# A window-attention kernel: new lead-in, an instruction order that counts tiling changes, deadlines for the small jobs, and the final add on GpSimd

## The chip, the core and the metric

The kernel runs on one core of one Trainium2 chip. The metric is the device time of one execution in microseconds; before the change it was 1138.44 us (median of three runs, 1138.19 to 1139.52). The profiles are single executions; their span (first to last instruction) is about two microseconds shorter than the time of the same execution.

## The reference

The image has 224 x 224 tokens of 96 channels. Half of the channels attend in horizontal stripes of 8 rows, the other half in vertical stripes of 8 columns: 28 + 28 windows of 1792 tokens, 48 channels each.

```python
qkv = jnp.einsum('bhwc,cd->bhwd', x, wqkv)
q, k, v = (qkv[..., :C].copy(), qkv[..., C:2 * C].copy(), qkv[..., 2 * C:].copy())
...
ah = _softmax(jnp.einsum('bqc,bkc->bqk', qh, kh) * scale, axis=-1)   # 28 horizontal windows
oh = jnp.einsum('bqk,bkc->bqc', ah, vh).reshape(B, H, W, C2)
...
av = _softmax(jnp.einsum('bqc,bkc->bqk', qv, kv) * scale, axis=-1)   # 28 vertical windows
...
return jnp.einsum('bhwc,cd->bhwd', o, wo)      # o: oh in the first 48 channels, ov in the others
```

## The kernel before

Two windows are computed side by side (a pair): 14 horizontal pairs, then 14 vertical ones. Every pair has 49 score tiles of 128 x 1024, so there are 1372. Each is made by PE (QK, in 64-row tiling, two windows x two column halves), turned into weights by either ACT (one exponential) or DVE (five instructions that build the bits of a bfloat16 exponential), and used by PE (PV, in 128-row tiling). PE also does the "fills": projections to K, Q and V, and the output projection. DVE copies their results out of PSUM ("evacuates" them), where the kernel has one tensor, `ps`, that PE writes and that is used in eight parts of 512 columns, the banks; only the first pair's Q goes through ACT.

The kernel has no dynamic scheduling. While it is built, a small model of the engines (`add` with an occupancy for each instruction) plays the program through and decides the order on each engine, including which tile goes to DVE. The order is then frozen; on the chip every engine works through its own list, waiting where a semaphore tells it to.

```python
        def add(eng, waits, fn, occ=100.0, done=None):
            ...
            start = max([now[0], tfree[eng]] + [vis(w) for w in waits])
            tfree[eng] = start + occ
            ...
        # ACT: one tile
            e = add("act", [ev, bufA_ev[sl]], lambda e, base=base, sl=sl: e.activation(
                PTA[sl][:], ps[:, base * 512:(base + 2) * 512], ACTF.Exp, scale=LN2 / 128.0), 912.0, 1200.0)
        # DVE: one tile, five steps; steps 1 and 3 are fp16 multiplies of two SBUF tiles
            if k == 0:
                return lambda e: e.tensor_scalar(tt_sb[:], dps.bitcast(U16)[:, 0:2048:2], CS / 65536.0, CS * CA3, ALU.mult, ALU.add)
            if k == 1:
                return lambda e: e.tensor_tensor(sq_sb[:], tt_sb[:], tt_sb[:], ALU.mult)
            if k == 2:
                return lambda e: e.tensor_scalar(sq_sb[:], sq_sb[:], CB, None, ALU.add)
            if k == 3:
                return lambda e: e.tensor_tensor(tt_sb[:], sq_sb[:], tt_sb[:], ALU.mult)
            return lambda e: e.scalar_tensor_tensor(PTD[sl][:].bitcast(U16), dps, CC, tt_sb[:], ALU.add, ALU.add)
        # PE takes another job only if it is over before the next QK for ACT can start
            def fits(occ):
                return nextfree is None or t + occ <= nextfree + SLACK or nextfree - t > 1500.0
        # last step of a vertical window, for each of up to five 128-token pieces s, on DVE
                            return e.scalar_tensor_tensor(out_sb[b][:, wdw, k0 + s, :], bk3[:, s, 0:C], rci[:, s:s + 1],
                                                          Ph_sb[:, k0 + s, j, :], ALU.mult, ALU.add)
```

The softmax here doesn't subtract the row's maximum and nothing guards it: scores larger than these inputs give would overflow.

## Time and profile before

Lines of the page of the kernel before. A group's line gives: source line, engine, operation, tiles, shape, count, then busy time and the mean length of one instruction in ns, then the engine's idle time just before them and what ended it. PEclk is the granted PE clock in tenths of full speed, in 40 slices of the span.

```profile
span 1137.3 us, 27720 instructions
...
PE 1023.0 (90%) x11824; PEld 372.9 (33%) x11824; DVE 1088.1 (96%) x2024; ACT 1110.5 (98%) x1206; POOL 1.6 (0%) x9
...
PEclk9999999999999999999999999999999999999999
...
ACT 68%; DVE 20%; PE 9%; SPq 2%; issue 1%; DMA 0%; DVEq 0%
...
L731 ACT ACTIVATE PTA<-ps 128x1024 bf16<-128x1024 f32 x1200 | 1106.6, 1087 | 7.9 <-PE ps L587 6.0
...
L742 DVE TENSOR_SCALAR tt_sb<-ps 128x1024 f16<-128x1024 uint16 x172 | 209.6, 1219 | 12.5 <-PE ps L587 10.8
L749 DVE SCALAR_TENSOR_TENSOR PTD<-ps,tt_sb 128x1024 uint16<-128x1024 f32 x172 | 209.7, 1219 | 1.9
...
L748 DVE TENSOR_TENSOR tt_sb<-sq_sb,tt_sb 128x1024 f16<-128x1024 f16 x172 | 118.5, 689 | 3.6
L744 DVE TENSOR_TENSOR sq_sb<-tt_sb 128x1024 f16<-128x1024 f16 x172 | 117.6, 684 | 0.8
...
L521 DVE SCALAR_TENSOR_TENSOR out_sb<-ps,rc,Ph_sb 128x96 bf16<-128x96 f32 x392 | 96.8, 308 | 1.0
L746 DVE TENSOR_SCALAR sq_sb<-sq_sb 128x1024 f16<-128x1024 f16 x172 | 72.2, 420 | 1.6
```

The five groups with count 172 are the five steps of the DVE tiles; L521 is the final step, five instructions in a row for a group of pieces. ACT is busy for 98% of the span and DVE for 96%. Lengths overlap in the pipeline: an exponential is listed with 1087 ns, but in the trace the most frequent distance from the start of one to the start of the next is 904 ns, which is ACT's real pace here.

The first exponentials, from the timeline of ACT (start, length of the merged stretch, how many):

```profile
14.75 0.64 ACT L392 ACTIVATE QT_sb<-ps,biasq 128x448 bf16<-128x448 f32 x1 [12.51 <-PE ps L369]
15.79 1.82 ACT L392 ACTIVATE QT_sb<-ps,biasq 128x448 bf16<-128x448 f32 x3 [0.40 <-PE ps L369]
17.55 1.94 ACT L731 ACTIVATE PTA<-ps 128x1024 bf16<-128x1024 f32 x2
19.78 1.94 ACT L731 ACTIVATE PTA<-ps 128x1024 bf16<-128x1024 f32 x2 [0.29 <-PE ps L587]
24.61 1.02 ACT L731 ACTIVATE PTA<-ps 128x1024 bf16<-128x1024 f32 x1 [2.89 <-PE ps L587]
26.18 12.08 ACT L731 ACTIVATE PTA<-ps 128x1024 bf16<-128x1024 f32 x13 [0.54 <-PE ps L587]
```

Nothing is exponentiated before 17.55 us, since all K and Q of the first pair are made first, and four microseconds later ACT runs dry again.

A split: the span is (number of exponentials) x 0.904 us plus the time ACT lost. The loss of one interval is the distance between two starts less 0.904 us, summed over the single instructions of the trace. For before: 1200 x 0.904 = 1084.8; until the first exponential 17.6; gaps up to 60 us 7.1; later intervals over 0.935 us lose 18.9, shorter ones 3.4; after the last 5.4. Sum 1137.2.

### The profile page before, as it was taken

The numbers are of one execution on the slowest core, as the hardware profiler recorded it, in microseconds if no ns is written. First come the engines' busy times: TensorE is split into PE (matmuls) and PEld (weight loads), VectorE is DVE, ScalarE is ACT, GpSimd is POOL, SyncE is SP. The second block draws the span as 40 slices with busy tenths as digits, with TensorE's granted clock in tenths as the row PEclk, the third lists the DMA queues.
The fourth block names the chain that finished last, engine by engine and source line by source line (L and its number), as shares of the span: only waits on it lengthen the run. The fifth ranks groups of instructions, "written<-read, shape, count | busy, mean of one in ns | idle before, by whom it ended". The sixth has DMA issues, their size and how long they took to land.

```text
span 1137.3 us, 27720 instructions
## 1 busy us (share of the span) xinstructions
PE 1023.0 (90%) x11824; PEld 372.9 (33%) x11824; DVE 1088.1 (96%) x2024; ACT 1110.5 (98%) x1206; POOL 1.6 (0%) x9
## 2 busy tenths in 40 slices
PE   5898899999999999999998898999899989999987
PEld 1333333333333333333333333333333333333332
DVE  3899999999999999999999999999999999999997
ACT  3999999999999999999999999999999999999998
POOL 0000000000000000000000000000000000000000
PEclk9999999999999999999999999999999999999999
DMA  4311011101100110110111222222122222221111
GB/s 83 54 34 34 10 26 34 34 1 33 35 19 16 33 34 5 30 31 16 21 34 33 40 42 40 38 41 41 38 40 42 40 40 43 40 39 26 19 27 25
DMA packets 169124, 37.31 MB, mean 33 GB/s; under 512 B 169000, under 2 KB 169000, under 8 KB 169000
## 3 DMA queue, kind: packets, MB, share of 16 engines
q1 hardware_dynamic: 167384, 35.36, 16.2%
q8 instruction: 92, 1.51, 0.6%
q10 hardware_dynamic: 1616, 0.18, 0.1%
q14 instruction: 32, 0.26, 0.1%
HBM read 0.15 MB, written 9.63 MB: 9 GB/s over the span
## 4 chain that ended last, share of the span: by engine, by line
ACT 68%; DVE 20%; PE 9%; SPq 2%; issue 1%; DMA 0%; DVEq 0%
ACT PTA L731 68%; PE ps L587 4%; DVE tt_sb L742 4%; PE ps L691 3%; DVE out_sb L521 3%; DVE PTD L749 3%; DVE sq_sb L744 2%; DVE tt_sb L748 2%; SPq L143 2%; DVE QT_sb L396 1%; DVE sq_sb L746 1%; DVE OT_sb L759 1%; DVE KT_sb L420 1%; DVE Ph_sb L482 1%; PE ps L369 1%
## 5 line engine op out<-in xcount | busy, mean ns | idle before, releaser
L731 ACT ACTIVATE PTA<-ps 128x1024 bf16<-128x1024 f32 x1200 | 1106.6, 1087 | 7.9 <-PE ps L587 6.0
L587 PE MATMUL ps<-QT_sb,KT_sb 49*64 49x512 bf16 (+3 forms) x6272 | 540.6, 370 | 81.3 <-ACT PTA L731 71.6
L691 PE MATMUL ps<-PTA,V_sb 128*64 128x512 bf16 (+1 forms) x2734 | 405.4, 365 | 1.4 <-DVE V_sb L337 0.4
L587 PEld LDWEIGHTS ps<-QT_sb,KT_sb 49*64 49x64 bf16 (+1 forms) x6272 | 157.1, 104 | 453.2 <-ACT PTA L731 382.8
L742 DVE TENSOR_SCALAR tt_sb<-ps 128x1024 f16<-128x1024 uint16 x172 | 209.6, 1219 | 12.5 <-PE ps L587 10.8
L749 DVE SCALAR_TENSOR_TENSOR PTD<-ps,tt_sb 128x1024 uint16<-128x1024 f32 x172 | 209.7, 1219 | 1.9
L691 PEld LDWEIGHTS ps<-PTA,V_sb 128*64 128x64 bf16 x2734 | 119.0, 108 | 150.0 <-issue 129.5
L748 DVE TENSOR_TENSOR tt_sb<-sq_sb,tt_sb 128x1024 f16<-128x1024 f16 x172 | 118.5, 689 | 3.6
L744 DVE TENSOR_TENSOR sq_sb<-tt_sb 128x1024 f16<-128x1024 f16 x172 | 117.6, 684 | 0.8
L369 PE MATMUL ps<-xT_sb,w_sb 128*64 128x448 bf16 (+1 forms) x448 | 85.5, 381 | 18.6 <-DMA xT_sb<-in_x_dram 9.9
L521 DVE SCALAR_TENSOR_TENSOR out_sb<-ps,rc,Ph_sb 128x96 bf16<-128x96 f32 x392 | 96.8, 308 | 1.0
L746 DVE TENSOR_SCALAR sq_sb<-sq_sb 128x1024 f16<-128x1024 f16 x172 | 72.2, 420 | 1.6
L396 DVE TENSOR_SCALAR QT_sb<-ps,biasq 128x448 bf16<-128x448 f32 x108 | 73.0, 676 | 0.4
L759 DVE CAST OT_sb<-ps 128x512 bf16<-128x512 f32 x112 | 68.9, 616 | 3.5 <-PE ps L691 3.5
L691 PE MATMUL ps<-PTD,V_sb 128*64 128x512 bf16 (+1 forms) x402 | 66.8, 353 | 2.7 <-DVE QT_sb L396 2.3
L420 DVE TENSOR_SCALAR KT_sb<-ps,shift 128x448 bf16<-128x448 f32 x84 | 56.6, 676 | 1.8 <-PE ps L369 1.6
L337 DVE CAST V_sb<-ps 128x480 bf16<-128x480 f32 (+1 forms) x84 | 51.5, 615 | 2.2 <-PE ps L330 2.2
L482 DVE TENSOR_TENSOR Ph_sb<-ps,rc 128x480 bf16<-128x480 f32 x84 | 52.0, 619 | 1.1
L369 PEld LDWEIGHTS ps<-xT_sb,w_sb 128*64 128x64 bf16 (+1 forms) x448 | 25.3, 108 | 72.5 <-issue 25.6
L471 PE MATMUL ps<-wo_sb,OT_sb 128*64 128x97 bf16 x784 | 33.0, 212 | 2.5 <-DMA wo_sb<-one_sb 1.6
L510 PE MATMUL ps<-wo_sb,OT_sb 128*128 128x97 bf16 x392 | 32.9, 210 | 2.2 <-DVE OT_sb L759 1.2
L330 PE MATMUL ps<-w_sb,xT_sb 128*128 128x48 bf16 (+1 forms) x784 | 34.1, 185 | 0.7 <-DVE V_sb L337 0.4
(33 smaller groups left out, 168.1 us busy)
## 6 DMA issues: line engine op xcount, KB each, us to landing
out_dram<-out_sb SPq DMA_DIRECT2D x389, 24.0 KB, 1.9
xT_sb<-in_x_dram SPq DMA_TRANSPOSE x336, 2.5
w_sb<-in_wqkv_dram ACTq DMA_DIRECT2D x2, 54.0 KB, 2.9
out_dram<-out_sb ACTq DMA_DIRECT2D x3, 24.0 KB, 1.9
wo_sb<-in_wo_dram SPq DMA_DIRECT2D x4, 9.0 KB
wo_sb<-one_sb SPq DMA_DIRECT2D x4, 0.0 KB
```

The lines of the kernel that those rows point to most:

```text
L369: ins = e.matmul(o, lhsT=wS[0:kr, wblk(P, kind), :], rhs=x_cols(wdw), start=True, stop=True)
L396: return e.tensor_scalar(q_dst, q_src(bk), QS, biasq[:, 0:1], ALU.mult, ALU.add)
L521: return e.scalar_tensor_tensor(out_sb[b][:, wdw, k0 + s, :], bk3[:, s, 0:C], rci[:, s:s + 1], Ph_sb[:, k0 + s, j, :], ALU.mult, ALU.add)
L587: ins = e.matmul(bank(base + wdw)[64 * kh:64 * kh + 64, i * qs:(i + 1) * qs], lhsT=KT_sb[b][r0:r0 + kk, kt * 128 + 64 * kh:kt * 128 + 64 * ...
L691: ins = e.matmul(bk[64 * wdw:64 * wdw + 64, 0:qs], lhsT=V_sb[b][:, wdw, kt, :], rhs=pt[:, wdw * 512 + i * qs:wdw * 512 + (i + 1) * qs], st ...
L731: e = add("act", [ev, bufA_ev[sl]], lambda e, base=base, sl=sl: e.activation(PTA[sl][:], ps[:, base * 512:(base + 2) * 512], ACTF.Exp, sca ...
L742: return lambda e: e.tensor_scalar(tt_sb[:], dps.bitcast(U16)[:, 0:2048:2], CS / 65536.0, CS * CA3, ALU.mult, ALU.add)
L744: return lambda e: e.tensor_tensor(sq_sb[:], tt_sb[:], tt_sb[:], ALU.mult)
L746: return lambda e: e.tensor_scalar(sq_sb[:], sq_sb[:], CB, None, ALU.add)
L748: return lambda e: e.tensor_tensor(tt_sb[:], sq_sb[:], tt_sb[:], ALU.mult)
L749: return lambda e: e.scalar_tensor_tensor(PTD[sl][:].bitcast(U16), dps, CC, tt_sb[:], ALU.add, ALU.add)
L759: ev = add("dve", [e_pv], lambda e: e.tensor_copy(OT_sb[b][:, q0:q0 + qs], bank(bi)[:, 0:qs]), t_ps(qs), t_ps(qs) + 150.0)
```

## The change

The intent: start the exponentials sooner; take the final add from DVE, which is as full as ACT, so that it can take more tiles; make the order model truer, so that gaps of ACT close. The core of the diff (cut):

```diff
+    SWITCH = 100.0
+    SLACK = 120
+    PACE = 1
+    FDUE = 25.0
+    DSLACK = 300.0
...
+            if mode is not None:
+                if mode != pe_mode[0]:
+                    start += SWITCH
+                pe_mode[0] = mode
+            if eng == "act" and start > tfree[eng]:
+                start += 17.0
...
-        for i in range(8):
+        for i in range(12):          # warm-up matmuls
...
+                    cuts = [0, 512, NTOK] if P == 0 else [k * 448 for k in range(5)]
...
-                q0, qs = c * PCH, PCH
+                q0, qs = (CH_Q0[c], CH_SIZES[c]) if P == 0 else (c * PCH, PCH)
...
-                return Fill(waits, pe_fn, 50.0 * n + 40.0, [dict(fn=ev_fn, occ=t_ps(n * C2))], post,
+                return Fill(waits, pe_fn, 25.0 * n, [dict(fn=ev_fn, occ=t_ps(n * C2))], post,
...
+                    def d2(e, bk):
+                        return e.tensor_tensor(tmpi[:, 0:n, :], bk3[:, 0:n, 0:C],
+                                               rci[:, 0:n].unsqueeze(2).to_broadcast([128, n, C]), ALU.mult)
...
+                        def d3(e):
+                            return e.tensor_tensor(out_sb[b][:, wdw, k0:k0 + n, :], tmpi[:, 0:n, :],
+                                                   Ph_sb[:, k0:k0 + n, j, :], ALU.add)
+                        if tail[0]:
+                            ev = add("dve", ow, d3, t_ps(n * C), t_ps(n * C) + 90.0)
+                        else:
+                            ev = add("pool", ow, d3, 2.3 * n * C + 150.0)
...
-            def fits(occ):
-                return nextfree is None or t + occ <= nextfree + SLACK or nextfree - t > 1500.0
-
-            if D["cur"] is None and fits(245.0):
+            def fits(occ, mode="r128", slack=SLACK):
+                if mode != pe_mode[0]:
+                    occ += SWITCH
+                if mode != "r64":
+                    occ += SWITCH
+                return nextfree is None or t + occ <= nextfree + slack or nextfree - t > 1500.0
+
+            if D["cur"] is None and fits(240.0, "r64", DSLACK):
...
-            late = want_fill and progress() > f.target + 2 and used < NBA - 1
+            late = want_fill and progress() > f.due - 10 and used < NBA - 1
...
-                PTA[sl][:], ps[:, base * 512:(base + 2) * 512], ACTF.Exp, scale=LN2 / 128.0), 912.0, 1200.0)
+                PTA[sl][:], ps[:, base * 512:(base + 2) * 512], ACTF.Exp, scale=LN2 / 128.0), 904.0, 1195.0)
...
-                    for i, f in enumerate(seq):
-                        f.target = P * NG + 1 + i * (NG - 14.0) / len(seq)
+                    for i, f in enumerate(order):
+                        f.target = P * NG + PACE * i
+                        f.due = P * NG + NG - LOOK - 18 + 2 * i
```

## The prediction

> **What bounds it now.** The page: ACT 1110.5 us busy (98% of 1137.3) and DVE 1088.1 (96%); PE is at 90%. The chain of waits is 68% the exponential on ACT. There are 1372 score tiles: 1200 go to ACT, 172 to DVE. Start to start in the trace, an exponential takes 904 ns at best; a DVE tile takes about 3.98 us over its five instructions. The span splits into 1200 x 0.904 = 1084.8 us, plus 52.5 us in which ACT lacks work:
> - lead-in: first exponential at 17.55 us, and about 7 us of gaps before 60 us (PE stood on the second pair's x);
> - steady part: about 22 us of small gaps (some 130 intervals over 0.95 us);
> - tail: 5.2 us after the last exponential.
>
> **Costs of the change.**
> 1. Lead-in. K and Q of the first pair wait for two transposes, not all. A transpose takes the queue 1.3 us at 448 tokens and 1.4 at 224, so nearly a fixed cost (estimate): the first pieces are issued by 3.3 us and land near 5.5 (eight landed at 12.6). Twelve warm-up matmuls at 0.43 us hold PE to about 6.6 us and become the limit. From the first K matmul to the first exponential the dependent work is about 2.6 us (4.9 now, as all K and Q came first): first exponential near 9.2 us. Lead-in loss falls from about 24.5 to 12.5 us.
> 2. Final add. On DVE 392 instructions (96.8 us; 1.21 a group of five) become 92 multiplies, 480 wide as a rule; the same shape takes 0.57 us in the first phase. DVE saves about 44 us and loses some 3 to the first pair (Q there, OT in pieces). GpSimd gets some 85 adds[...].
> 3. Order model with tiling changes, deadlines, earlier QK for DVE: ACT gaps in the steady part fall from 22 to about 15 us, DVE idles about 5 us less.
>
> **Sum.** ACT and DVE share the tiles, so DVE time is worth only 0.904/(3.98+0.904) = 0.185 us a us; an ACT gap 0.815. With non-tile DVE time (work and idle) going from 452 to about 410 us, and ACT loss from 52.5 to about 33: 1.227 T = 1240.3 + 33 + 0.227 x 410, T = 1113.5 us of span, about 176 DVE tiles; the time is 1 us more.
>
> **Prediction:** 1114 us, 1103 to 1124; faster by over 2%: 0.55, within 2%: 0.44, slower: 0.01.
>
> **What would show it.** First exponential at 8-10.5 us; 174 to 182 DVE tiles; multiply near 0.6 us; [...]intervals of the exponential over 950 ns clearly fewer; the fp16 instructions longer in the second half only where GpSimd overlaps.
>
> **What would make it wrong.** GpSimd locking DVE out (few more tiles, fp16 steps over 1 us); a 1280-token transpose whose cost grows with size (K of the rest after 11 us); the new order filling more gaps than I think (1105).

Parts of step 2 and one sign are cut: how long one of GpSimd's adds takes, and with it how long GpSimd would be busy; which DVE steps its reads would hold up; and a booking for that, 12 us of DVE loss, possibly 0 to 40. None of them was worked out from a trace or a run; the 12 us was a guess, and it was noted then that no run had shown the loss. The sum came to a span of T = 1113.5 us, with about 410 us of DVE time outside tiles. The terms that are left give 406 (452 - 44 + 3 - 5), with the cut 12 us 418; at 0.227/1.227 = 0.185 us a us the 12 us are 2.2 us of T, so the forecast does not hang on them.

## More of the kernel before

The PE clock is at nine tenths of full speed or more in every slice; after the lead-in this execution has one stretch at half clock, 3.4 us at 40.9 us.

What PE waited for most in front of QK (total us, times, longest):

```profile
PE ps L587 <- ACT PTA L731: 71.6, 229, 0.5
...
PE ps L587 <- DVE PTD L749: 4.2, 15, 0.4
```

PE waits for ACT, as it should where ACT is the limit. It hardly waits for PTD, the last step of a DVE tile, which frees the banks for the next DVE tile.

## The result, and the profile after

The changed kernel took 1142.10 us (median of 4, 1140.92 to 1142.73) against 1138.98 us for before beside it: ratio 1.0024, 95% interval 1.0007 to 1.0042. A ratio is the mean time of one kernel's fast runs over that of the other's of the same rounds, so it is not quite the ratio of the medians. The 2% gain that I thought slightly more likely than not did not come, and 1142 lies far outside 1103 to 1124.

The page of the changed kernel:

```profile
span 1139.9 us, 27621 instructions
...
PE 1044.0 (92%) x11828; PEld 372.0 (33%) x11828; DVE 1078.8 (95%) x1746; ACT 1106.9 (97%) x1201; POOL 94.4 (8%) x99
...
PEclk8999999799999999999999999979999999999999
...
ACT 66%; DVE 22%; PE 8%; issue 3%; DMA 0%; SPq 0%; POOL 0%
...
L780 ACT ACTIVATE PTA<-ps 128x1024 bf16<-128x1024 f32 x1198 | 1104.7, 1214 | 22.3 <-PE ps L635 20.5
...
L791 DVE TENSOR_SCALAR tt_sb<-ps 128x1024 f16<-128x1024 uint16 x174 | 212.4, 1221 | 20.9 <-PE ps L635 18.2
L798 DVE SCALAR_TENSOR_TENSOR PTD<-ps,tt_sb 128x1024 uint16<-128x1024 f32 x174 | 212.0, 1219 | 1.7
L573 POOL TENSOR_TENSOR out_sb<-tmp,Ph_sb 128x480 bf16<-128x480 f32 (+2 forms) x90 | 92.8, 1031 | 1039.5 <-DVE tmp L558 1039.5
...
L797 DVE TENSOR_TENSOR tt_sb<-sq_sb,tt_sb 128x1024 f16<-128x1024 f16 x174 | 134.9, 775 | 3.3
L793 DVE TENSOR_TENSOR sq_sb<-tt_sb 128x1024 f16<-128x1024 f16 x174 | 119.6, 687 | 0.2
...
L795 DVE TENSOR_SCALAR sq_sb<-sq_sb 128x1024 f16<-128x1024 f16 x174 | 77.7, 446 | 2.9
...
L558 DVE TENSOR_TENSOR tmp<-ps,rc 128x480 f32<-128x480 f32 (+2 forms) x92 | 53.1, 577 | 0.8
```

Three things stand out. PEclk shows sevens, which the forecast did not have. PE has no more work than before (11828 matmuls against 11824, four more of them warm-up); it is listed as busier because a matmul takes longer at half clock (the 49x512 of QK 631 ns, 400 at full clock, medians). The second multiply (L797) grew from 689 to 775 ns on average. And only 174 tiles are on DVE, the low end of the 174 to 182 forecast, although 392 instructions of the final step are gone.

The start of ACT came as forecast, even a little earlier:

```profile
6.43 0.69 ACT L429 ACTIVATE QT_sb<-ps,biasq 128x512 bf16<-128x512 f32 x1 [2.65 <-PE ps L403]
8.16 1.94 ACT L780 ACTIVATE PTA<-ps 128x1024 bf16<-128x1024 f32 x2 [1.04 <-PE ps L635]
11.90 2.85 ACT L780 ACTIVATE PTA<-ps 128x1024 bf16<-128x1024 f32 x3 [1.80 <-PE ps L635]
15.24 1.02 ACT L780 ACTIVATE PTA<-ps 128x1024 bf16<-128x1024 f32 x1 [0.49 <-PE ps L635]
16.81 1.02 ACT L780 ACTIVATE PTA<-ps 128x1024 bf16<-128x1024 f32 x1 [0.54 <-PE ps L635]
18.38 27.61 ACT L780 ACTIVATE PTA<-ps 128x1024 bf16<-128x1024 f32 x30 [0.54 <-PE ps L635]
```

The first exponential is at 8.16 us, the steady stream begins at 18.4.

PE's waits in front of QK again:

```profile
PE ps L635 <- ACT PTA L780: 61.3, 216, 0.8
PE ps L635 <- DVE PTD L798: 12.9, 22, 1.1
```

PE now stands 12.9 us on the last step of DVE tiles, 4.2 before. One such case, from the timeline of all engines:

```profile
731.05 0.65 DVE L558 TENSOR_TENSOR tmp<-ps,rc 128x480 f32<-128x480 f32 x1
...
731.62 0.42 DVE L795 TENSOR_SCALAR sq_sb<-sq_sb 128x1024 f16<-128x1024 f16 x1
731.78 1.20 POOL L573 TENSOR_TENSOR out_sb<-tmp,Ph_sb 128x480 bf16<-128x480 f32 x1 [20.90 <-DVE tmp L558]
...
732.08 1.47 DVE L797 TENSOR_TENSOR tt_sb<-sq_sb,tt_sb 128x1024 f16<-128x1024 f16 x1
...
733.57 1.23 DVE L798 SCALAR_TENSOR_TENSOR PTD<-ps,tt_sb 128x1024 uint16<-128x1024 f32 x1
...
734.85 0.63 PE L635 MATMUL ps<-QT_sb,KT_sb 50*64 50x512 bf16 x8 [0.74 <-DVE PTD L798]
```

GpSimd's add starts at 731.78. The multiply that DVE starts at 732.08 takes 1.47 us instead of 0.69 and ends 0.57 us after the add (732.98), as if it had begun only then. The last step follows late, and PE, which has the next DVE tile's QK at the head of its list, stands 0.74 us for it. Split over the whole trace: 28 of these multiplies overlap an add and occupy DVE (start to end, less what overlaps the next instruction) for 1183 ns on average, the other 146 for 630. The third step, which has one SBUF input, is longer too: 547 ns in the 29 cases beside an add, 387 in the others; the first multiply took 675 ns in 11 cases beside an add, 645 in the others. The two steps with a PSUM input show no such lengthening: the first step took 1139 ns with an add (34 cases) and 1143 without, the last 1163 with (17 cases) and 1136 without. The lengthening of DVE's steps beside an add is called the lock below.

Now the clock. The trace records when the granted PE clock is 1.0 and when 0.5. In the changed kernel it is 0.5 in four stretches of 3.4 or 13.7 us, 34 us together, starting at 213.2, 742.3, 834.4 and 868.6 us. Stretches of the trace just before, and in, the two long ones (busy us and number of instructions by engine, then granted clock, DMA share and GB/s):

```profile
core 0: us, PE busy (x) PEld busy (x) DVE busy (x) ACT busy (x) POOL busy (x), PEclk, DMA share, GB/s
209.80:213.20 3.40, 2.05 (x30) 0.72 (x26) 2.64 (x5) 3.40 (x5) 0.00 (x0) 1.00 0.00 0
213.20:226.80 13.60, 13.53 (x92) 3.51 (x88) 6.54 (x10) 9.87 (x11) 0.00 (x0) 0.50 0.15 31
738.90:742.30 3.40, 2.09 (x24) 0.62 (x22) 3.37 (x5) 3.05 (x4) 0.40 (x1) 1.00 0.26 50
742.30:755.90 13.60, 13.41 (x78) 3.16 (x74) 10.25 (x20) 9.58 (x10) 2.91 (x3) 0.50 0.20 39
```

In the 3.4 us before the clock fell PE was busy for about 2.05 us only (a typical share is nine tenths), with no idle gap over 0.51 us in the first of them; before the two short stretches it was busy for 2.38 and 2.26 us. In the 13.6 us at half clock, ACT gets 11 and 10 exponentials done where 15 fit.

The split of the span, with the prediction worked into the same terms (us):

| term | before | after | predicted |
|---|---|---|---|
| exponentials x 0.904 | 1084.8 (1200) | 1083.0 (1198) | about 1081 (1196) |
| until the first exponential | 17.6 | 8.2 | 9.2 |
| gaps up to 60 us | 7.1 | 4.2 | about 3 |
| gaps in half-clock stretches after 60 us | 0 | 13.8 | not foreseen |
| other gaps after 60 us | 22.3 | 24.7 | 15 |
| after the last exponential | 5.4 | 6.1 | 5.5 |
| sum | 1137.2 | 1140.0 | about 1114 |

Of the intervals over 0.935 us outside half-clock stretches, those before 580 us lost 8.2 us before and 2.6 after; those later lost 10.7 before and 15.2 after. GpSimd's adds begin at 607 us.

The planner's own end time, which the kernel computes while it is built, makes the point sharp: 1113.8 us before, 1095.6 after. The plan got 18 us better; the chip ended 23.5 us behind the plan before, and 44.3 after.

### The profile page after: what moved, and what is told of

Its sections match the earlier page's. It is cut to its first block, busy times and chain, and to the rows that moved or that the text cites. A ratio compares the mean times of both kernels' runs of the same rounds, so it can differ in the third digit from the quotient of the medians.

```text
span 1139.9 us, 27621 instructions
## 1 busy us (share of the span) xinstructions
PE 1044.0 (92%) x11828; PEld 372.0 (33%) x11828; DVE 1078.8 (95%) x1746; ACT 1106.9 (97%) x1201; POOL 94.4 (8%) x99
## 4 chain that ended last, share of the span: by engine, by line
ACT 66%; DVE 22%; PE 8%; issue 3%; DMA 0%; SPq 0%; POOL 0%
ACT PTA L780 66%; DVE tt_sb L791 5%; DVE tt_sb L797 4%; PE ps L635 4%; DVE PTD L798 4%; PE ps L743 3%; DVE tmp L558 3%; DVE sq_sb L795 2%; DVE QT_sb L433 2%; DVE OT_sb L825 1%; DVE sq_sb L793 1%; DVE KT_sb L457 1%; DVE V_sb L372 1%; PE ps L403 1%; DVE rc L552 0%
## 5 line engine op out<-in xcount | busy, mean ns | idle before, releaser
L780 ACT ACTIVATE PTA<-ps 128x1024 bf16<-128x1024 f32 x1198 | 1104.7, 1214 | 22.3 <-PE ps L635 20.5
L743 PE MATMUL ps<-PTA,V_sb 128*64 128x512 bf16 (+1 forms) x2742 | 428.4, 370 | 0.7 <-ACT PTA L780 0.3
L791 DVE TENSOR_SCALAR tt_sb<-ps 128x1024 f16<-128x1024 uint16 x174 | 212.4, 1221 | 20.9 <-PE ps L635 18.2
L798 DVE SCALAR_TENSOR_TENSOR PTD<-ps,tt_sb 128x1024 uint16<-128x1024 f32 x174 | 212.0, 1219 | 1.7
L573 POOL TENSOR_TENSOR out_sb<-tmp,Ph_sb 128x480 bf16<-128x480 f32 (+2 forms) x90 | 92.8, 1031 | 1039.5 <-DVE tmp L558 1039.5
L797 DVE TENSOR_TENSOR tt_sb<-sq_sb,tt_sb 128x1024 f16<-128x1024 f16 x174 | 134.9, 775 | 3.3
L403 PE MATMUL ps<-xT_sb,w_sb 128*64 128x448 bf16 (+3 forms) x448 | 86.0, 381 | 4.9 <-DVE OT_sb L825 2.0
L433 DVE TENSOR_SCALAR QT_sb<-ps,biasq 128x448 bf16<-128x448 f32 (+2 forms) x111 | 75.1, 677 | 5.8 <-PE ps L403 5.6
L795 DVE TENSOR_SCALAR sq_sb<-sq_sb 128x1024 f16<-128x1024 f16 x174 | 77.7, 446 | 2.9
L825 DVE CAST OT_sb<-ps 128x512 bf16<-128x512 f32 (+5 forms) x118 | 69.3, 592 | 2.8 <-PE ps L743 2.6
L457 DVE TENSOR_SCALAR KT_sb<-ps,shift 128x448 bf16<-128x448 f32 (+2 forms) x84 | 56.8, 676 | 3.8 <-PE ps L403 3.8
L558 DVE TENSOR_TENSOR tmp<-ps,rc 128x480 f32<-128x480 f32 (+2 forms) x92 | 53.1, 577 | 0.8
```

What stands on the lines that cost most here:

```text
L403: ins = e.matmul(o, lhsT=wS[0:kr, wblk(P, kind), :], rhs=x_cols(wdw), start=True, stop=True)
L433: return e.tensor_scalar(q_dst, q_src(bk), QS, biasq[:, 0:1], ALU.mult, ALU.add)
L558: return e.tensor_tensor(tmpi[:, 0:n, :], bk3[:, 0:n, 0:C], rci[:, 0:n].unsqueeze(2).to_broadcast([128, n, C]), ALU.mult)
L573: return e.tensor_tensor(out_sb[b][:, wdw, k0:k0 + n, :], tmpi[:, 0:n, :], Ph_sb[:, k0:k0 + n, j, :], ALU.add)
L743: ins = e.matmul(bk[64 * wdw:64 * wdw + 64, 0:qs], lhsT=V_sb[b][:, wdw, kt, :], rhs=pt[:, wdw * 512 + i * qs:wdw * 512 + (i + 1) * qs], st ...
```

## The experiments

Theory A: two things that the plan does not know took the gain. GpSimd's reads lock DVE out (1183 against 630 ns for the second multiply), and in a frozen order a late DVE tile holds up PE (12.9 us in all) and then ACT. And the new order leaves stretches in which PE does little; after such a stretch (2.05 to 2.38 us busy of 3.4 above) the clock is halved. Rival B: the order is simply too tight for the chip. Rival C: the clock falls because PE's work is denser.

Most of what is compared below are differences under 2%. "Half clock" counts the time at clock 0.5 in the profiled run alone, between 30 us and 15 us before its end (the expectations count to the end, so theirs is larger, 103 us for the add on DVE); ratios are against before in the same rounds.

| run | median us | ratio | DVE tiles | half clock us |
|---|---|---|---|---|
| before (profile shown above) | 1138.98 | 1 | 172 | 3.4 |
| the change | 1142.10 | 1.0024 | 174 | 34.1 |
| e1_pool_writes_only | 1132.27 | 0.9924 | 174 | 27.3 |
| e2_qk_twice | 1143.71 | 1.0016 | 174 | 45.4 (slow run) |
| e3_add_on_dve | 1173.30 | 1.0262 | 161 | 95.6 |
| e4_lead_only | 1132.93 | 0.9933 | 171 | 0 |
| e5_lead_gpsimd | 1148.14 | 1.0100 | 178 | 6.8 |
| e6_lead_gpsimd_gated | 1125.59 | 0.9882 | 178 | 0 |
| e7_gated | 1135.25 | 0.9970 | 174 | 20.5 |
| e8_dve_no_tiling | 1136.26 | 0.9978 | 169 | 6.8 |
| e9_dve_qk_twice_where_thin | 1144.32 | 1.0046 | 161 | 8.1 |
| e10_gated_qk_twice_where_thin | 1127.49 | 0.9896 | 174 | 0 |
| e11_gated_tiling_50 | 1124.63 | 0.9863 | 176 | 5.3 |
| e12_gated_tiling_0 | 1130.89 | 0.9919 | 176 | 0 |

### GpSimd only writes (wrong result)

```diff
                         else:
+                            def d3(e):
+                                return e.memset(out_sb[b][:, wdw, k0:k0 + n, :], 0.0)
                             ev = add("pool", ow, d3, 2.3 * n * C + 150.0)
```

> Same instruction order on every engine as the changed kernel, but GpSimd only writes zeros where it added (result wrong on purpose). Theory A (GpSimd's reads lock DVE out, the late DVE tile holds up PE's queue, PE's thin stretch then halves its clock): the last fp16 multiply of a DVE tile (775 ns mean, 1183 ns where GpSimd overlaps it) goes back to about 690 ns mean; PE's wait for the PTD step falls from 12.9 us to 4-8; of the half-clock time after 570 us (20.5 us) at most 7 us is left, while the half-clock stretch near 213 us, before GpSimd's first add, stays; time 1124 to 1133 us. Rival B (the order itself is too tight, whatever GpSimd does): 1138 to 1143 us.

Measured: 1132.27 us (1127.67 to 1135.73), ratio 0.9924, with 0.9886 to 0.9962 as interval. The group lines of the second multiply and of what GpSimd did:

```profile
L799 DVE TENSOR_TENSOR tt_sb<-sq_sb,tt_sb 128x1024 f16<-128x1024 f16 x174 | 119.5, 687 | 3.3
...
L579 POOL MEMSET out_sb<- 128x480 bf16 (+2 forms) x90 | 44.8, 498 | 1073.2 <-DVE tmp L558 1073.2
```

The multiply is back at 687 ns although GpSimd still overlaps 28 of them (636 ns there, 631 elsewhere), and PE's wait for the last DVE step fell to 0.5 us, below the 4 to 8 forecast. Large gaps outside half-clock stretches fell from 17.8 to 5.3 us. The half-clock stretch at 213 us stayed, and 17 us came at 271 and 998 us instead of the three later ones, so the time ended inside the range forecast, but the forecast that the later half-clock stretches would mostly go was wrong: at most a part of them came from the lock. The same order, with the lock away, is about 10 us faster than the change. Two limits: GpSimd's instruction is also shorter (498 ns, 1031 for the add), and the four runs fall into two groups, near 1128 us with a granted clock of 0.984 and 0.985, and near 1136 with 0.974; the trace is of the first.

### QK issued twice in the four half-clock stretches

```diff
+            twice = kk == KA and any(lo <= len(qA) < hi for lo, hi in [(208, 232), (774, 797), (869, 883), (904, 918)])
-                for i, kt in enumerate(kts):
+                for i, kt in [x for x in enumerate(kts) for _ in range(2 if twice else 1)]:
```

> The changed kernel with the QK matmuls of 75 of 1198 ACT tiles issued twice, only in and just ahead of the four stretches where its PE clock was halved: more work for PE, same result. Theory A (a stretch of 3.4 us with little PE work halves the clock): the four stretches vanish or shrink, half-clock time after 30 us from 38 us (the last 4 us are the end of the program) to under 14, ACT's loss inside half-clock stretches from 13.8 us to under 4, time 1128 to 1135 us. Rival C (dense PE work brings the throttle): as much half-clock time or more, time 1142 us or above. Rival B: the stretches go, but other gaps take their place, time 1138 to 1142.

Measured: 1143.71 us (1140.07 to 1157.22; the slowest, which is the profiled one, counts as slow). None of the four places halved the clock in the profiled run, but the clock fell at 263 and 1017 us and stayed at half for the last 44 us. As it is a slow run, nothing is concluded from its trace. The three fast runs (1140.07 to 1145.01 us) had a granted clock of 0.986 to 0.992, the change 0.979 to 0.983: more clock, but no gain (ratio 1.0016 against 1.0024). For theory A it is a miss; it speaks against rival C, and what rival B had forecast (1138 to 1142 us) comes nearest.

### The add back on DVE, all else as in the change

```diff
-                      [dict(fn=d1, occ=85.0), dict(fn=d2, occ=t_ps(n * C), waits=w2)], post,
+                      [dict(fn=d1, occ=85.0)] + [mk_d(s) for s in range(n)], post,      # five multiply-adds as before
```

> The changed kernel with the final step of before (five multiply-adds on DVE per group) in place of GpSimd's add. Its own plan says 161 DVE tiles and 1114 us against 174 and 1096 for the changed kernel. Theory A: no DVE instruction is lengthened; what the plan loses (18 us) is partly given back (no GpSimd lock, fewer late DVE tiles): 1133 to 1143 us, DVE tile steps as in before. If GpSimd's lock cost more than the add saved, under 1130; if GpSimd cost nothing, above 1150.

Measured: 1173.30 us, 30 us above the range. The steps of DVE tiles are all at their length of before (second multiply 687 ns, third step 421, last step 1218; 689, 420 and 1219 in before), so the lock is gone, yet the clock was at half for 95.6 us in 14 stretches, and the loss of ACT in them is 37.6 us. So in this kernel the trouble sits in the new order itself, and a lock is not needed for it. This told me that I had weighed theory A's two halves wrongly. The reading for a time above 1150, that GpSimd costs nothing, does not follow either: it left the clock out, and the three kernels without the lock (above and below) are 7 to 23 us faster than the same ones with it.

### The lead-in alone

Before's order rules and final step, with the new lead-in; against the change, the other parts are undone:

```diff
-    SWITCH = 100.0
+    SWITCH = 0.0
-    DSLACK = 300.0
+    DSLACK = 120.0
... (912 ns, occupancies of the fills, targets, choice of the next fill, and the final step as in before)
```

> Before with the new lead-in alone (old order rules, old final step on DVE). First exponential near 8.2 us, 171 DVE tiles planned, no half-clock stretch longer than 4 us outside the ends. Theory A: the lead-in is sound and was outweighed by the rest: 1124 to 1131 us, 8 to 14 us below before. Rival (the tighter start shifts later work and gives the gain back): 1134 to 1140 us.

Measured: 1132.93 us (two runs near 1131, two near 1135), ratio 0.9933 (0.9907 to 0.9959), first exponential at 8.31 us, no half-clock stretch between the lead-in and the last microsecond in the profiled run (clock 0.995; the two runs near 1135 had 0.988 and were not traced). The lead-in is worth about 7.3 us, a little less than forecast.

### Lead-in and GpSimd's add, old order; and the same with the adds gated

The gate is the second diff. The add is planned behind the second multiply of a DVE tile, so that it runs beside the two steps that read PSUM:

```diff
-                            ev = add("pool", ow, d3, 2.3 * n * C + 150.0)
+                                ev = add("pool", ow + [gate_ev], d3, 2.3 * n * C + 150.0)   # planned by put(), kept in held
...
                     d["k"] += 1
+                    if k == 3 and held:
+                        held.pop(0)((ev[0], ev[1], ev[2] - 80.0))
```

> Before with the new lead-in and the add on GpSimd, old order rules. Plan: 178 DVE tiles, 1100 us (the lead-in alone planned 1107, measured 1132.9). Theory A: GpSimd's lock costs DVE about 20 us again (last fp16 multiply about 1.2 us where GpSimd overlaps), and since the order is fixed ahead, ACT loses more in gaps in the second half than the lead-in alone did: 1128 to 1136 us, so little or nothing of the 7 us planned arrives. If the order rules are the sole cause, and the lock harmless, 1123 to 1128.

> As the run with lead-in and GpSimd's add, with each add made to wait until the second fp16 multiply of a DVE tile is done, so that it runs beside the two PSUM-reading steps that follow. Theory A: DVE steps that GpSimd overlaps go back to their usual length (fp16 multiply 0.63 us), ACT's gaps in the second half are as in the lead-in alone: 1120 to 1128 us, the best so far. If GpSimd's lock does not matter, the same as the ungated one within 3 us.

Measured: 1148.14 us ungated, 1125.59 us gated (1124.00 to 1126.75; ratio 0.9882, 0.9864 to 0.9899). The ungated one is worse than I had expected even under theory A. Both have the same 178 DVE tiles and the same plan (1100.2 us). The second multiply's line, ungated:

```profile
L796 DVE TENSOR_TENSOR tt_sb<-sq_sb,tt_sb 128x1024 f16<-128x1024 f16 x178 | 144.4, 811 | 3.7
```

and gated:

```profile
L806 DVE TENSOR_TENSOR tt_sb<-sq_sb,tt_sb 128x1024 f16<-128x1024 f16 x178 | 123.1, 691 | 3.7
```

Summed without overlaps, the five steps of the 178 tiles took 725.5 us ungated and 702.6 gated, 23 us less. The time differs by 22.6 us. So here the lengthening of DVE by the lock went almost in full into the time. In the traces, ACT's gaps after 60 us outside half clock are 42.3 us ungated and 23.7 gated; the ungated run also lost 3.8 us in a half-clock stretch of 6.8 us, which the gated one does not have. Beside a gated add the last step took 1137 ns (78 cases), without one 1140.

### The change, gated

The gate of the previous section in the changed kernel (`SWITCH = 100.0` and all else kept).

> The changed kernel with GpSimd's adds gated in the same way, result correct. Should be like the run in which GpSimd only wrote (1132.3 us): 1127 to 1137 us, no DVE step lengthened by GpSimd, PE's wait for the PTD step at 4 to 8 us, half-clock stretches still there (10 to 35 us).

Measured: 1135.25 us, ratio 0.9970. The DVE steps are unlengthened (687.2 us for 174 tiles, 3.95 us each; 3.94 in before); PE's wait for the last DVE step 0.5 us, even less than forecast; 20.5 us at half clock, 17.1 of it before 570 us. Without the lock and with a right result, the change still loses 9.7 us of ACT in half-clock stretches.

Two comparisons follow. Against the change, the gate took 19.4 us from the DVE steps (706.6 to 687.2) and 11.0 us from ACT's gaps outside half clock (24.7 to 13.7), but only 6.9 us from the time. In this order a microsecond of lock cost about a third of a microsecond of time, not one. And against e6_lead_gpsimd_gated, which has the same lead-in and the same gated add but the old order rules, this run is 9.7 us slower (ratios 0.9970 and 0.9882 in the same rounds): as they stand in the change, the new order rules cost time.

### The count of tiling changes set to zero, add on DVE

```diff
-    SWITCH = 100.0
+    SWITCH = 0.0
```

> The kernel with the add on DVE (1173.3 us, 103 us at half clock, 161 DVE tiles) with the cost of a tiling change in the order model set to 0 instead of 100 ns, all else of the new order kept: 169 DVE tiles planned, plan 1098 us. If counting tiling changes is what thins PE's work out: under 30 us at half clock and 1125 to 1140 us. If the deadlines of the fills are: still over 70 us at half clock and 1155 us or more.

Measured: 1136.26 us against 1173.30 with the count. Half clock 6.8 instead of 95.6 us, 169 DVE tiles instead of 161. So with the deadlines kept, it is the counting of tiling changes that both thins PE's work out and keeps tiles away from DVE (the count without the deadlines was not run). The remaining new rules (deadlines, 904 ns, shorter fills) gain nothing on top of the lead-in: ratio 0.9978 here, 0.9933 for the lead-in with the old rules.

The count is not wrong as a fact. In the traces, the start of a QK group's last matmul and the start of a following PV lie 330 ns apart, a PV and a following QK 309, a PV and a fill of the same tiling 236 (medians). By these differences (309 and 330 less 236) a change costs 70 to 95 ns in these traces. What it does to the order is the trouble: `fits` (in the code above) now asks up to 200 ns more for a PV or fill between two QKs, and such work is put off until PE has little but QK left.

### QK issued twice wherever the plan is thin

The test of the clock, on the slowest kernel and on the gated change. PE gets more to do; the order is the same.

```diff
+            while pe_log and pe_log[0] < now[0] - 3413.0:
+                pe_log.pop(0)
+            twice = kk == KA and now[0] > 12000.0 and len(pe_log) < 10    # groups planned in the last 3.4 us
```

> The slowest kernel so far (new order, add on DVE: 1173.3 us, 103 us at half clock) with one addition: where fewer than ten groups of PE work were planned in the last 3.4 us, the next ACT tile's QK is issued twice into the same bank (224 of 1211 tiles, some 48 us more PE work, same order otherwise, same result). Theory A (too little PE work in a stretch halves the clock): under 35 us at half clock after 30 us, 1130 to 1148 us. If the low clock came from something else, or the stretches were its effect only: over 80 us at half clock and 1165 us or more.

> The changed kernel with gated GpSimd adds (1135.3 us) and the same doubling of QK where the plan is thin (191 tiles). Theory A: no half-clock stretch over 4 us between 30 and 1110 us, ACT's loss there from 9.7 to under 3 us: 1122 to 1130 us. If the extra PE work costs as much as the clock: 1133 to 1140.

Measured: 1144.32 instead of 1173.30 us, and 1127.49 instead of 1135.25. The second half of the slowest kernel, and 120 us of it, first as it was (same columns as in the stretches above):

```profile
580.00:1120.00 540.00, 495.83 (x5184) 167.97 (x5184) 472.34 (x982) 515.76 (x557) 0.00 (x0) 0.93 0.18 35
840.00:960.00 120.00, 109.93 (x1088) 35.84 (x1084) 92.68 (x191) 109.04 (x117) 0.00 (x0) 0.86 0.19 36
```

and with QK doubled in 224 of 1211 tiles:

```profile
580.00:1120.00 540.00, 509.54 (x5973) 179.40 (x5969) 493.40 (x1025) 535.84 (x584) 0.00 (x0) 1.00 0.18 36
840.00:960.00 120.00, 113.45 (x1330) 39.86 (x1328) 104.19 (x219) 119.11 (x130) 0.00 (x0) 1.00 0.20 40
```

PE does a fifth more matmuls in the 120 us (a tenth more for each exponential, as the kernel also gets further), the clock is 1.00 instead of 0.86, and ACT gets 130 exponentials done instead of 117. Extra work without any use made the kernel 29 us faster (ratio to before 1.0046 instead of 1.0262), and the gated change 7.8 us. Rival C falls. Rival B is not the main cause in the slowest kernel, but it does not fall; see the next section.

The granted clocks of the runs, which need no trace, fit. Within one kernel, a run with 10 us more at half clock (an estimate: twice what the mean clock lacks to 1, times the span) took 3.1 us longer (50 fast runs of the change and the twelve kernels made from it, each against its kernel's mean; correlation 0.97). Before's own 21 runs beside them do not show it: 1137.6 to 1142.0 us at clocks from 0.988 to 1.000, without a relation. That half clock costs little where ACT does not wait for PE would explain it, but this is not shown.

How little work came before a fall can be counted. I divided all 14 traces into windows of 3.41 us, the length of the two shorter half-clock stretches of the change (its longer two are four times as long), and took the array time of the matmuls started in each. This is an estimate, since a few records are missing: elements streamed at 2.4 per ns, the pace of matmuls back to back at full clock in these traces (512 elements in 213 ns), divided by the number of matmuls that fit side by side by their rows and columns (four of QK start within 10 ns of each other, two of PV within 4). Of some 4100 full-clock windows with a share of 0.50 or more, none was followed by half clock; of 17 under 0.38, 15 were; of some 40 between 0.38 and 0.44, 14; of some 190 between 0.44 and 0.50, 2.

### The tiling change counted at 50 ns, and not at all, with gated adds

```diff
-    SWITCH = 100.0
+    SWITCH = 50.0        # 0.0 in the second
```

> The changed kernel, gated, with the tiling change counted at 50 ns instead of 100: 176 DVE tiles planned. Between the two neighbours: 1124 to 1134 us, half-clock time after 30 us under 25 us.

> The changed kernel, gated, with the tiling change not counted: 176 DVE tiles planned, 1092 us. If the count of tiling changes is what thins PE's work out, half-clock time after 30 us under 12 us and 1122 to 1130 us, with ACT's larger gaps back at about 20 us in all (5 us in the gated kernel that counts them). If the fills' deadlines thin it: as the gated kernel, 1133 to 1138, over 20 us at half clock.

Measured: 1124.63 us (1121.61 to 1126.56; ratio 0.9863, 0.9842 to 0.9884) and 1130.89 us, 0.9 us above the range forecast. With 0 there is no half clock, but the larger gaps of ACT are back at 22.9 us; at 100 they are 5.1 us, with 20.5 us at half clock; at 50 they are 12.5, with 5.3 us at half clock. So the count does close gaps, as it was meant to, and pays for it with the clock; the middle is better than both ends. This version and the gated one with the old order beat both kernels, by 1.2 to 1.4% of before, still under 2%; their intervals overlap, so which of the two is better is open.

What is left of rival B: with the count at 0 there is neither lock nor half clock, and yet this kernel is 5.3 us slower than the gated one with the old rules (1130.89 and 1125.59 us, in different rounds; ratios 0.9919 and 0.9882, with intervals that do not touch). Its span ends 35.5 us behind its plan of 1092 us; with the old rules the gated kernel ends 24 us behind (1123.8 against 1100), the lead-in alone 22 (1129.0 against 1107), before 23.5. So the new rules make a plan that the chip follows less well, whatever the lock and the clock do; which of their shorter occupancies or deadlines does it was not tested.

## Why the prediction was wrong

- **What bounds the kernel: right.** ACT's pace of 904 ns, the count of tiles and the split of the rest held in every run.
- **Step 1, the lead-in: right.** "Lead-in loss falls from about 24.5 to 12.5 us": it fell from 24.7 to 12.4. That the sum is so exact is luck: the first exponential came 1.0 us earlier than forecast, and the gaps up to 60 us were 1.2 us larger. The transpose is nearly a fixed cost indeed: 1.22 and 1.25 us of the queue for 512 tokens, 1.52 and 1.50 for 1280 in the trace of the change. Alone it gave 7.3 us between the medians.
- **Step 2, the final add: the saving right, its loss mis-valued.** "DVE saves about 44 us and loses some 3": the work of DVE outside tiles fell from 409.7 to 371.7 us, 38. The booking of 12 us of DVE loss, a guess: against the per-tile length of before (677.7 / 172 = 3.940 us) the steps of the 174 tiles were 21 us longer, inside the 0 to 40 that went with it. GpSimd's adds took 1.09 to 1.54 us for 480 elements (52 of them, median 1.10), 94 us of GpSimd in all. What failed here is the term in the sum: "DVE time is worth only 0.904/(3.98+0.904) = 0.185 us a us". That exchange rate is true in the plan, where a free microsecond can be given to another tile. The lock is not in the plan. It comes after the order is frozen, so nothing is shared out anew: DVE is late, PE stands at the head of its list (12.9 us in the change, 0.5 with the gate), ACT runs dry. With the old order rules the gated and ungated pair shows 22.6 us of time for 23 us of DVE, a rate near 1; in the change itself the gate brought 6.9 us of time for 19.4 us of DVE, a rate of 0.35. Both are well above 0.185, and they differ, so no single rate is shown.
- **Step 3, the order model: the step with the largest error.** It left the clock out. "ACT gaps in the steady part fall from 22 to about 15 us": they rose from 22.3 to 38.5, 24.7 of it outside half-clock stretches. Without the lock the part outside half clock does fall (13.7 us in the gated change, 13.6 where GpSimd only wrote), so the direction was right for that part, but the half-clock stretches take it back (9.7 and 11.0 us). But I took the granted clock of before, 1.0 but for one stretch of 3.4 us, as given for the new order, and it was not: 34 us at half clock cost ACT 13.8 us. Worked out from the prediction's own rates, this step was to gain some 6 to 7 us of time (an estimate: 7 x 0.815 + 5 x 0.185); the gated pair with old and new rules shows a loss of 9.7. I also thought that better order would only help DVE; counting tiling changes cost 8 DVE tiles (169 against 161 with the add on DVE).
- **The sum.** The loss of ACT was to be 33 us and was 56.9: 13.8 from half clock, 9.7 more from other gaps, most of it in the second half where the lock is, 0.6 in the tail. Two tiles fewer on DVE are another 1.8 us. This is a split of one trace and not what taking out each cause gives back: the gate gave 6.9 us, more PE work another 7.8, and at 1127.49 us the kernel was still 13 us over the forecast.
- **What I had named as ways to fail:** the lock was named, its price was not; the clock was not named at all. The signs under "What would show it" all came (8.16 us; 174 tiles; 577 ns; 104 intervals over 950 ns, 144 before; the second multiply 1183 ns beside an add, 630 elsewhere), and the time did not: they tested the parts that were right.

What stays open: why the clock stays at half for 3.4 us after some thin stretches and for 13.7 or more after others, and what exactly counts as PE work for it; how much of the later half-clock time of the change came from the lock; and why the chip ends further behind the plan with the new rules even where neither is at work.

## What to carry to other kernels

Where the order is frozen ahead, do not value a slowdown that the planner does not know at the rate at which the planner could share it out (0.185 here; 0.35 to 1 was measured); and take the slowdown out by timing (here GpSimd's adds beside DVE steps that read PSUM: last step 1137 ns with an add, 1140 without; 22.6 us less time with the old order, 6.9 with the new). In these kernels PE was not the limit (ACT was busy for 97% of the changed kernel's span), and its clock still fell where it had little to do: look at the granted clock of the changed kernel before believing any gain, and check each stretch of some 3.4 us of the plan for a minimum of matmul work (here no half clock followed a window with a share of 0.50 or more, by the estimate above). A truer cost in a model is no gain by itself if the rule that uses it has nothing in it against the thing that then goes wrong.
